# Talking-heads attention and squared-ReLU FFN: other anchors for the q, k and v loads, the first k by SP, some pre-mixing units in row tiles, and a new order of TensorE's units

## Chip, cores and metric

One core of one Trainium2 chip. The metric is the device time of one launch in microseconds (us), as the median of the runs shown; lower is better. Beside these runs stands one profiled execution, whose own time is given with its span.

## What is computed

Attention over 8 batches, 12 heads, 448 positions and a head size of 64, with the heads mixed before the softmax (`w_pre`) and after it (`w_post`), then a feed-forward layer with a squared ReLU on the 3584 x 768 result:

```python
scores = scale * np.matmul(q, k.transpose(0, 1, 3, 2))
scores = np.einsum('bhij,hg->bgij', scores, w_pre)
scores = scores - np.max(scores, axis=-1, keepdims=True)
attn = np.exp(scores)
attn = attn / (np.sum(attn, axis=-1, keepdims=True) + 1e-09)
attn = np.einsum('bhij,hg->bgij', attn, w_post)
return np.matmul(attn, v).astype(np.float32)
...
h = np.maximum(x @ w_in, 0.0)
return (h * h @ w_out).astype(np.float32)
```

Inputs and output are float32; the kernel computes in bfloat16 with float32 sums.

## The kernel before

**The stages of a batch.** q and k come from DRAM as bfloat16 (POOL's queue, `load_qk`, L624, two DMAs of half the partitions for each of three head groups `a` and each of q and k), and TensorE transposes them (`emit_T`, L710; "T" units). QK units (`emit_QK`, L859) give the scores of 128 query rows at a time, which ACT or DVE evict into `stage`; SP's DMAs (`emit_rel`, L918) regroup them in `dring` so that 10 query rows times 12 heads lie on the partitions. A pre-mixing unit (`emit_pre`, L940) multiplies two such groups by the block-diagonal `wk1`; ACT takes the exponentials with row sums into `pring` (L965), DVE the reciprocals, POOL folds them into the post-mixing weights (L986) and the tail (L1001). A post-mixing unit (`emit_post`, L1014) gives the mixed and transposed attention, evicted into `a2t`. AV units (`emit_AV`, L1092) multiply by v, F1 units (`emit_F1`, L1163) and F2 units (`emit_F2`, L1282) are the feed-forward layer. The output leaves from `osb` by POOL's queue, except the last two tiles (`emit_last`, L1242), which leave by SP and ACT.

**Batch 0 is different.** The first 22 groups of 10 rows skip regrouping and pre-mixing: DVE multiplies the transposed q by the mixing weights (`emit_scale`, L788; the products lie in `w_out_sb` and `h2t`, not yet in use), and "direct" units (`emit_direct`, L814) make mixed scores at once. Until 60 us, TensorE's gaps are partly filled by matmuls on a constant (`warm_up`, L587).

**TensorE's tiles.** A matmul uses the whole array ("full"), two tiles of 64 rows ("row"), two of 64 columns ("cols") or four of 64 x 64 ("quad"). Pre-mixing and T units are quad, post-mixing units and most QK units row, AV units cols, direct units full; F1 and F2 are row or full by a string each. In a pre-mixing unit each of the four tiles runs one 448-column matmul at the same time as the others.

**What sets the order.** The whole program is planned ahead: `_Plan` (L108) gives each task an engine and a place in that engine's queue. TensorE's units stand in ten streams (0 T, 1 QK, 2 pre-mixing, 3 post-mixing, 4 AV, 5 direct, 6 and 7 F1, 8 and 9 F2), and the string `ORDER` (L32), 948 digits long, says from which stream the next unit comes. All other tasks are placed by estimated costs and by a priority. A dependency in `deps` becomes a semaphore wait; one in `after` only keeps the planner from issuing a task before another, and leaves no wait in the program. The loads of batch b >= 2 are tied in this way to pre-mixing units (`emit_load_qk`, L678, and `emit_load_v`, L695, by `pre_at`): the twelve q and k loads to every second group from group 2 of batch b - 1, the six v loads to every second group from group 8 of batch b itself. The raw buffers are single, so each load also waits for the T unit of the batch before. The planner's constants (`FETCH` for instruction fetches of TensorE, `MODE_SWITCH`, `MARGIN` for the time kept free behind a transfer) enter nothing but its estimates.

Of the kernel before, what the change touches and what calls it, by code (L numbers as in the profile page):

```python
# [8 lines left out]
DT = mybir.dt  # L9
# [9 lines left out]
MODE_SWITCH = 106.0  # L19
ACT_BIAS = 14.5  # L20
BLOCK = 256
FETCH = (110e3, 6000.0, 4600.0, 1400.0)
# [6 lines left out]
MARGIN = {("move", PE): (0.0, 700.0), ("move", FLEX): (700.0, 1500.0),  # L29
          ("load", PE): (0.0, 900.0)}  # L30
INF = float("inf")
ORDER = (  # L32
    "0010155055051505511551555115555113553155550033555555550105555555311553332550220555315551"
    "2313332431244123622317667223677313361372267113667313242244137611376713127721266676623336"
    "7277128310028323839139229839200223444132622008111811181338317222167663123776313673132621"
    "4431411367217127766327621002677622383383338162267720028332677102208311813181338314212442"
    "2229391139313933922291444229119116316337221763363372217620016733722631620027137383200281"
    "1181118222939133911393124222441183138311831382224442216363372217633637212763362002277200"
    "2611637337339200292219119118131813183318222444223931193139331922244422881383138336221672"
    "1276200167337136336222772002736316720209119313922193831183138113822244422381381338224442"  # L40
    "2816336117117336221673373621167200226731362002713783382228382002911392219139393319222931"
    "9318338111811382224444442236171163377331722166662227637336372127922198338392298333832244"
    "42228876323267886673363363676787774448687787766676697767689989889999"
# [3 lines left out]
QK_QUAD = "001000000001000000000000000000000000000000001001000000010000001000000000000000000000000000000000000000000000000000000000000000000000000000000000000000000000000"  # L47
POST_QUAD = "0000000000000000000000000000000000000000000000000000000000000000000000000000000000000000000000000000000000000000000000000000000000000000000000000000000000000000000000000000000001100000"

# [58 lines left out]
class _Plan:  # L108
# [191 lines left out]
    def next_unit(self, order, at):  # L300
# [8 lines left out]
        if t.mode != self.mode:  # L309
            est = max(est, self.free[PE] + MODE_SWITCH)  # L310
# [41 lines left out]
def bass_talking_heads_attention__then__ffn_squared_relu_kernel(  # L352
# [45 lines left out]
    with ExitStack() as es:  # L398
# [883 lines left out]
        def emit_F2(b, tile, s, s_F):  # L1282
# [10 lines left out]
            if b == B - 1 and tile >= 2:  # L1293
                emit_last(b, tile, s, s_F, _Group(2), reads)
                return
# [185 lines left out]
```

## Time and profile before

| | |
|---|---|
| runs | 518.51, 519.75, 520.62 us; median 519.75 |
| profiled execution | 520.99 us, of it 519.3 us span |
| granted TensorE clock | 1.0 |
| TensorE (PE) busy | 506.3 us, 98% of the span |
| ACT, DVE, POOL busy | 434.1, 401.9, 268.4 us |
| DMA | 72.33 MB moved, HBM read 47.27 MB |

The profile names engines PE (matmuls), PEld (weight loads, overlapped), DVE, ACT, POOL and SP; a line such as L948 is a line of the kernel. "idle before" is the time an engine stood still ahead of an instruction, with the one that ended it. In the view of windows, each row is a stretch of the span, followed by the busy time of each engine and its number of instructions, the granted clock, the mean busy share of 16 DMA engines and GB/s. In a timeline, a row is a start, a length, an engine, a line and what was done, with equal neighbours merged.

### The profile page before, as it was taken

To read this page: it belongs to the slowest core of one execution; us is meant where nothing else is said; L and a number is where in the kernel's file an instruction comes from. 1 tells how busy PE (TensorE), PEld (TensorE's weight loads), DVE (VectorE), ACT (ScalarE), POOL (GpSimd) and SP (SyncE) were. 2 spreads that over 40 slices of the span, in tenths; PEclk is the share of its full clock that TensorE was granted. 3 is DMA by queue.
4 is the path that set the end of the run, shared out by engine and by line. 5 is a ranking of instruction groups with operands and counts; after the bars stand their busy time and mean duration, and the time that the engine had idled before them with its cause. 6 is when DMAs were issued, how large, how long until landed. Compare 5 with 4: busy or idle time off the path is not lost.

```text
span 519.3 us, 22377 instructions
## 1 busy us (share of the span) xinstructions
PE 506.3 (98%) x9169; PEld 319.7 (62%) x9169; DVE 401.9 (77%) x1025; ACT 434.1 (84%) x1256; POOL 268.4 (52%) x571
## 2 busy tenths in 40 slices
PE   7999899999999999999999999999999999999997
PEld 3455677567776664567455664566545665568884
DVE  8998999689979769888988869886896668755220
ACT  4989999799999898988888889888998888987531
POOL 9956556443673576244864459235664344443000
PEclk9999999999999999999999999999999999999999
DMA  8999999846895689646993679626995466551013
GB/s 112 196 227 193 199 180 189 168 115 136 157 190 135 142 174 187 124 97 141 173 186 76 142 156 197 148 66 152 174 166 119 102 154 120 103 118 32 1 32 93
DMA packets 83022, 72.33 MB, mean 139 GB/s; under 512 B 7160, under 2 KB 80424, under 8 KB 82920
## 3 DMA queue, kind: packets, MB, share of 16 engines
q0 software_dynamic: 37632, 33.83, 40.4%
q1 hardware_dynamic: 45000, 36.86, 29.0%
q8 instruction: 74, 1.21, 0.9%
q14 instruction: 28, 0.23, 0.1%
q10 hardware_dynamic: 288, 0.20, 0.1%
HBM read 47.27 MB, written 11.01 MB: 112 GB/s over the span
## 4 chain that ended last, share of the span: by engine, by line
PE 73%; DVE 12%; ACT 8%; DMA 3%; issue 2%; POOL 2%; POOLq 0%; ACTq 0%; DVEq 0%
PE ps L1311 23%; PE ps L1184 10%; PE ps L1176 10%; PE ps L1120 6%; PE ps L948 6%; PE ps L879 5%; PE ps L1036 5%; ACT pring L965 4%; PE ps L1303 3%; DVE stage L487 3%; DVE a2t L487 2%; PE ps L1251 2%; DMA kraw<-in_k_dram 2%; DVE w_out_sb L802 2%; PE ps L726 2%; ACT stage L486 2%
## 5 line engine op out<-in xcount | busy, mean ns | idle before, releaser
L965 ACT ACTIVATE pring<-ps 128x448 bf16<-128x448 f32 x360 | 191.7, 557 | 11.7 <-PE ps L948 9.4
L986 POOL TENSOR_TENSOR wk2s<-wk2b,rinv 128x120 bf16<-128x120 bf16 (+1 forms) x179 | 73.2, 409 | 145.7 <-DVE rinv L979 144.3
L487 DVE CAST a2t<-ps 128x420 bf16<-128x420 f32 (+1 forms) x208 | 124.8, 643 | 16.5 <-PE ps L1050 15.9
L1311 PE MATMUL ps<-w_out_sb,h2t 64*128 64x384 bf16 x1472 | 134.3, 323 | 0.3 <-ACT pring L965 0.2
L487 DVE CAST stage<-ps 128x448 bf16<-128x448 f32 (+1 forms) x179 | 107.3, 615 | 14.1 <-PE ps L879 12.8
L486 ACT ACTIVATE a2t<-ps 128x420 bf16<-128x420 f32 (+1 forms) x160 | 94.9, 645 | 13.1 <-PE ps L1050 12.8
L486 ACT ACTIVATE stage<-ps 128x448 bf16<-128x448 f32 (+1 forms) x181 | 94.8, 557 | 12.9 <-PE ps L879 12.2
L1311 PEld LDWEIGHTS ps<-w_out_sb,h2t 64*128 64x128 bf16 x1472 | 67.6, 94 | 45.3 <-issue 2.4
L1184 PE MATMUL ps<-xt,w_in_sb 64*128 64x448 bf16 (+1 forms) x840 | 88.4, 347 | 1.3 <-issue 1.1
L1348 POOL DMA_DIRECT2D out_dram<-osb x52 | 33.4, 648 | 93.3 <-ACT osb L486 30.7
L965 ACT ACTIVATION_READ_ACCUMULATOR pring<-ps 128x1 f32 x360 | 80.0, 222 | 0.0
L1176 PE MATMUL ps<-xt,w_in_sb 128*128 128x228 bf16 (+2 forms) x636 | 75.0, 270 | 1.0 <-ACT a2t L486 0.8
L1223 DVE TENSOR_TENSOR h2t<-h1t 128x448 bf16<-128x448 bf16 (+2 forms) x176 | 56.0, 341 | 20.2 <-ACT h1t L1213 17.1
L1001 POOL TENSOR_TENSOR ptail<-pring,rinv 128x128 bf16<-128x128 bf16 x171 | 70.2, 410 | 0.0
L1176 PEld LDWEIGHTS ps<-xt,w_in_sb 128*128 128x128 bf16 x636 | 58.2, 98 | 13.9 <-ACT a2t L486 1.7
L1036 PEld LDWEIGHTS ps<-wk2s,pring 60*128 60x128 bf16 (+1 forms) x2184 | 48.9, 94 | 24.7 <-issue 2.6
L1184 PEld LDWEIGHTS ps<-xt,w_in_sb 64*128 64x128 bf16 x840 | 37.5, 94 | 34.8 <-issue 2.2
L1213 ACT ACTIVATE h1t<-ps 128x448 bf16<-128x448 f32 (+2 forms) x100 | 43.5, 445 | 16.6 <-PE ps L1176 7.6
L1036 PE MATMUL ps<-wk2s,pring 60*128 60x60 bf16 (+1 forms) x2184 | 55.3, 187 | 1.3 <-ACT h1t L1213 0.6
L948 PE MATMUL ps<-dring,wk 64*64 64x448 bf16 (+1 forms) x676 | 54.0, 362 | 0.9 <-DVE a2t L487 0.3
L979 DVE RECIPROCAL rinv<-rowsum 128x2 f32<-128x2 f32 (+1 forms) x184 | 29.0, 157 | 32.9 <-ACT pring L965 31.5
L879 PE MATMUL ps<-qkt 64*128 64x448 bf16 (+1 forms) x372 | 51.1, 353 | 0.4 <-DVE qkt L487 0.3
(62 smaller groups left out, 564.1 us busy)
## 6 DMA issues: line engine op xcount, KB each, us to landing
dring<-stage SPq DMA_DIRECT2D x309, 105.0 KB
out_dram<-osb POOLq DMA_DIRECT2D x52, 192.0 KB, 4.0
vraw<-in_v_dram POOLq DMA_DIRECT2D x48, 128.0 KB
qraw<-in_q_dram POOLq DMA_DIRECT2D x48, 112.0 KB, 5.4
kraw<-in_k_dram POOLq DMA_DIRECT2D x48, 112.0 KB, 5.3
w_in_sb<-in_moe_w_in_dram POOLq DMA_DIRECT2D x8, 384.0 KB, 18.0
w_out_sb<-in_moe_w_out_dram POOLq DMA_DIRECT2D x8, 384.0 KB, 17.3
dring<-stage SPq DMA_DIRECT2D x30, 42.0 KB
```

The lines of the kernel that those rows point to most:

```text
L486: return eng.activation(o, i_, AF.Copy)
L487: return eng.tensor_copy(o, i_)
L879: r_ = eng.matmul(ps[y * v:(y + 1) * v, g.banks[x], 0:S], qkt[r0:r0 + 64, pp, 0, j0:j0 + v], qkt[r0:r0 + 64, pp, 1 + pb, :], start=True, s ...
L948: r_ = eng.matmul(ps[64 * y:64 * y + 64, gr.banks[x], 0:S], wk1[64 * x:64 * x + 64 - R0 * x, :], dring[64 * x:64 * x + 64 - R0 * x, (g0 + ...
L965: return eng.activation(pring[:, pr, 0:S], ps[:, gr.banks[x], 0:S], AF.Exp, accum_out=rowsum[:, pr, :])
L986: return eng.tensor_tensor(wk2s[:, p0:p0 + n, :], i0.to_broadcast([128, n, PR]), rinv[:, p0:p0 + n, :].to_broadcast([128, n, PR]), ALU.mult)
L1001: return eng.tensor_tensor(ptail[:, p0 // 2, :, :], pring[:, p0:p0 + 2, 0:PJ], rinv[:, p0:p0 + 2, :].to_broadcast([128, 2, PJ]), ALU.mult)
L1036: r_ = eng.matmul(ps[z * v:(z + 1) * v, gr.banks[x], o0:o0 + PR], pring[64 * x:64 * x + PR, pr + y, c:c + v], wk2s[64 * x:64 * x + PR, pr ...
L1176: r_ = eng.matmul(ps[:, gs[ph].banks[0], 0:n], w_in_sb[:, ft, t * 128:(t + 1) * 128], xt[:, ft, c0:c1], start=(ft == 0), stop=(ft == NFT - 1))
L1184: r_ = eng.matmul(ps[:, gs[0].banks[x], 0:n], w_in_sb[64 * y:64 * y + 64, ft, t * 128:(t + 1) * 128], xt[64 * y:64 * y + 64, ft, c0:c1], s ...
L1223: return eng.tensor_tensor(h2t[:, t16, o0:o0 + n], h1t[:, s, 0:n], h1t[:, s, 0:n], ALU.mult)
L1311: r_ = eng.matmul(ps[:, gs[0].banks[hh], 0:FH], h2t[64 * y:64 * y + 64, t16, col:col + 128], w_out_sb[64 * y:64 * y + 64, t16, hh * FH:(hh ...
```

## The change

- **Loads.** The q and k loads of batches 3 to 7 are tied to every second group from group 36 of batch b - 2 (46 group numbers a batch), so twelve groups earlier; batch 2 keeps its anchors. The v loads of batches 1 to 7 are tied to every third group from group 12 of their batch in place of every second from group 8.
- **First k.** Head group 0 of k of batch 0 no longer comes by POOL's queue with conversion on the way. SP issues two DMAs of float32 into the space of `pring` ahead of its other work, and ACT converts them into `kraw` (task "round").
- **Pre-mixing in row tiles.** For the units marked in `PRE_ROW` the same product is made by two passes of row tiles: each pass runs two 64-row tiles on 448 columns, the second adding to the first, with weights padded by zeros (`wk1z`). Ten units are marked: three of batch 0, three of batch 1 and one each of batches 2 to 5.
- **End.** The last output tile is cut in three instead of two: 384 columns, then twice 192, each with its own PSUM bank, eviction and two DMAs.
- **Plan.** `ORDER` and `QK_QUAD` (seven units in place of six) are new; `F1_FULL`, `F2_FULL` and `POST_QUAD` are the same. The planner's constants change: costs of a unit, of a change of tile mode, margins behind transfers, and a further one for fetches while several loads are in flight.

```diff
-MODE_SWITCH = 106.0
+MODE_SWITCH = {"quad": 119.0, "cols": 121.0, "row": 105.0, "full": 105.0}
-FETCH = (110e3, 6000.0, 4600.0, 1400.0)
+FETCH = (110e3, 6000.0, 4000.0, 5300.0, 1300.0)
-MARGIN = {("move", PE): (0.0, 700.0), ("move", FLEX): (700.0, 1500.0),
-          ("load", PE): (0.0, 900.0)}
+MARGIN = {("move", PE): (300.0, 1300.0), ("move", FLEX): (1000.0, 2200.0),
+          ("load", PE): (0.0, 1800.0)}
...
-        z = (at - self.fetched - FETCH[1 if at < FETCH[0] else 2]) / FETCH[3]
+        late = 1 if at < FETCH[0] else 3 if len(self.moving["load"]) > 1 else 2
+        z = (at - self.fetched - FETCH[late]) / FETCH[4]
...
+        def load_first_k():
+            wide = pring.bitcast(DT.float32)[:, 0:4, :].rearrange("p a b -> p (a b)")
+            ts = []
+            for u in range(2):
+                def fn(eng, en, u=u):
+                    i_ = bass.AP(k.tensor, u * NP * S * D, [[NT * D, PJ], [S * D, 2], [1, NT * D]])
+                    eng.dma_start(wide[64 * u:64 * u + 64, :].rearrange("p (a b) -> p a b", a=2),
+                                  i_).then_inc(sem_k.handle, 16)
+
+                ts.append(plan.add("ldk%d" % u, SP, fn, [], {SP: (420.0, 0.0)}, -2e6 + u,
+                                   sem_k, 16, dma=("load", 350.0, 88.0)))
+
+            def fn_round(eng, en):
+                o = kraw[:, 0:2, :, :].rearrange("p a t d -> p (a t d)")
+                return eng.activation(o, wide, AF.Copy)
+
+            t = add("round", ACT, fn_round, ts, {ACT: (985.0, 1135.0)}, -5e6)
+            return [t, t]
...
+                    if (b, a, x) == (0, 0, 1):
+                        ts += load_first_k()
+                        continue
...
-                            after = [chain["t"], pre_at((b - 1) * NCP + 2 + 2 * n)]
+                            g0 = (b - 1) * NCP + 2 if b == 2 else (b - 2) * NCP + 36
+                            after = [chain["t"], pre_at(g0 + 2 * n)]
...
-                after = [qk_tasks[(1, 2)][-1]] if b < 1 else [pre_at(b * NCP + 8 + 2 * n)]
+                after = [qk_tasks[(1, 2)][-1]] if b < 1 else [pre_at(b * NCP + 12 + 3 * n)]
...
+                if row:
+                    for y in (1, 0):
+                        for x in range(len(gs)):
+                            rows = slice(64 * x, 64 * x + 64 - R0 * x)
+                            c0, m = (0, 128) if y else (64, 66)
+                            r_ = eng.matmul(ps[0:m, gr.banks[x], 0:S], wk1z[rows, c0:c0 + m],
+                                            dring[rows, (g0 + y) % NDS, :],
+                                            start=y == 1, stop=True, skip_group_check=True)
+                    return r_
...
-            for hh in range(2):
-                for q0 in range(0, NFFT, nk):
+            spans = [(0, 0, 2, nk), (1, 2, 2, nk)]
+            if tile == 3:
+                spans = [(0, 0, 2, nk), (1, 2, 1, NFFT), (2, 3, 1, NFFT)]
+            for i, y0, ny, nu in spans:
+                w = ny * OP
...
-                emit_last(b, tile, s, s_F, _Group(2), reads)
+                emit_last(b, tile, s, s_F, _Group(tile), reads)
```

## What is predicted, before the changed kernel ran

> **What bounds the kernel now.** I read the profile by stages first, since TensorE's 98% is a mean over stages with different limits.
>
> ```profile
> 0.00:6.00 6.00, 4.54 (x42) 2.00 (x42) 4.20 (x10) 2.46 (x3) 4.84 (x13) 1.00 0.55 78
> 6.00:15.00 9.00, 7.33 (x183) 3.30 (x169) 8.67 (x23) 5.35 (x11) 8.99 (x16) 1.00 1.06 143
> 15.00:35.00 20.00, 20.00 (x269) 9.91 (x268) 19.92 (x52) 17.60 (x50) 16.43 (x23) 1.00 1.26 216
> 35.00:65.00 30.00, 27.85 (x525) 17.57 (x523) 26.56 (x71) 28.53 (x89) 17.99 (x40) 1.00 1.12 199
> 65.00:200.00 135.00, 133.56 (x2586) 92.64 (x2580) 113.32 (x305) 123.94 (x374) 77.72 (x168) 1.00 0.79 160
> 200.00:330.00 130.00, 127.70 (x2541) 75.75 (x2537) 111.70 (x272) 114.32 (x325) 71.41 (x156) 1.00 0.74 148
> 330.00:515.00 185.00, 184.65 (x3060) 118.31 (x3050) 117.53 (x299) 141.44 (x407) 71.05 (x159) 1.00 0.48 103
> 515.00:519.30 4.30, 0.71 (x5) 0.20 (x2) 0.00 (x0) 0.49 (x1) 0.00 (x0) 1.00 0.35 92
> ```
>
> The first number after the stretch is its length, the next TensorE's busy time, then weight loads, DVE, ACT, POOL, the clock, the DMA share and GB/s. TensorE's idle time is the difference of the first two: 1.46 and 1.67 us before 15 us, none from 15 to 35, 2.15 from 35 to 65, 1.44 to 200, 2.30 to 330, 0.35 to 515 and 3.59 in the tail, 12.96 in all. So better waiting can save at most some 13 us, and after 330 us almost nothing: there each nanosecond of added TensorE work adds to the end. Between 6 and 35 us DVE is full as well (28.59 of 29 us), though TensorE looks busy with matmuls on a constant among the rest.
>
> Next the start, by the timeline, and the chain of waits across it.
>
> ```profile
> 0.81 0.40 SPq L556 DMA_DIRECT2D wall<-in_w_pre_dram  x1
> 2.65 1.22 POOL L630 DMA_DIRECT2D kraw<-in_k_dram  x2
> 4.15 1.25 POOL L630 DMA_DIRECT2D qraw<-in_q_dram  x2
> 5.68 0.30 PEld L726 LDWEIGHTS ps<-ident,qraw 64*64 64x64 bf16 x28 [0.37 <-DMA qraw<-in_q_dram]
> 7.67 0.30 PEld L726 LDWEIGHTS ps<-ident,kraw 64*64 64x64 bf16 x28 [1.34 <-DMA kraw<-in_k_dram]
> 14.04 0.30 PEld L726 LDWEIGHTS ps<-ident,kraw 64*64 64x64 bf16 x28 [0.37 <-DMA kraw<-in_k_dram]
> ...
> 7.08 5.29 DMA qraw<-in_q_dram
> 13.28 1.70 DVE w_out_sb L802 x3
> ```
>
> The six tensors of batch 0 arrive one after the other: first q transposed at 5.68, last k at 14.04, that is (14.04 - 5.68) / 5 = 1.67 us apiece. The chain runs through POOL's issues and such a landing until 12.37 us and through DVE from there. The input transfers pace the first 12 us, DVE the next 23.
>
> **The change part by part.** *First k by SP.* The nearest rows for its price are SP's transfer of 72 KB and an ACT copy of as many columns:
>
> ```profile
> wall<-in_w_pre_dram SPq DMA_DIRECT2D x1, 72.0 KB, 3.4
> L486 ACT ACTIVATE qkt<-ps 128x896 bf16<-128x896 bf16 x5 | 4.6, 912 | 0.0
> ```
>
> Each of the two new loads is 64 x 2 x 1792 bytes, 229 KB. They stand first on SP, so the second is issued at 0.81 + 0.40 = 1.21 us. From below it lands like the 72 KB, at 4.6; from above 459 KB at the 216 GB/s of the busiest stretch add 2.1 us, 6.7. I take 5.3. ACT converts in some 0.91 us and is free (2.46 of 6 us busy), so k is ready at 5.5 to 7.6, most likely 6.2, and its transposes start then in place of 7.67. The matrix of mixing weights, queued behind on SP, is issued 0.8 us later; its first user on DVE comes only after 6 us, and it lands by 0.81 + 0.8 + 3.4 = 5.0, so it costs nothing. POOL issues 1.22 us less ahead of the second q, and one of six places in the row of landings is gone: the last input is there up to 1.67 us sooner. DVE has only 0.33 us idle in 6 to 15, so the gain comes through only as far as ACT (3.65 us idle there) takes over evictions. Ends 0 and -1.67; I take **-1.2**, near the second, as the chain has transfers until 12.37.
>
> *Loads of batches 3 to 7.* The first row is the landing of k's DMAs over the whole run (minimum, median, maximum).
>
> ```profile
> DMA to landing us min/median/max: 3.7/5.3/12.1
> 256.35 0.61 POOL L630 DMA_DIRECT2D kraw<-in_k_dram  x1
> 256.95 0.65 POOL L641 DMA_DIRECT2D vraw<-in_v_dram  x1
> 257.57 0.63 POOL L630 DMA_DIRECT2D kraw<-in_k_dram  x1
> 267.25 0.30 PEld L726 LDWEIGHTS ps<-ident,kraw 64*64 64x64 bf16 x28 [0.57 <-DMA kraw<-in_k_dram]
> ...
> 105.51 2.41 PE ps L1120 x60
> 257.57 9.63 DMA kraw<-in_k_dram
> ```
>
> Today q, k and v loads alternate on POOL, since their anchors overlap; a k issued at 257.57 landed 9.63 us later and TensorE stood 0.57 us. In the order string the last anchor of batch 3's third pair is 15 units ahead of its use; 948 units in 515 us are 0.54 us each, so that is 8 us, under the maximum of 12.1. With the new string the same distance is 41 units, 22 us. The waits on the raw buffers stay met: the T unit that frees one stands at least 36 units ahead of the new anchor in each of the batches 3 to 7, so nothing queued behind these loads on POOL (folds and tails, for which post-mixing waits) is held up by them. The number of DMAs stays but for the two of the first k. v's last anchor comes nearer to its first AV unit: 20 units (11 us) or more in batches 2 to 7, but in batch 1 it is 10 units, 5.4 us, where it was 29; the AV work of batch 1 is the row at 105.51. If that landing is like k's median it just fits (see the last rival). So **-0.5**, between -0.6 and the +6.7 of that rival.
>
> *Stalls without a cause in the program.* Twice TensorE stood in the middle of an F1 unit, both times while loads had just been issued:
>
> ```profile
> 205.66 0.63 POOL L630 DMA_DIRECT2D qraw<-in_q_dram  x1
> 206.83 0.30 PEld L1184 LDWEIGHTS ps<-xt,w_in_sb 64*128 64x128 bf16 x5 [1.18 <-issue]
> 256.69 0.68 PEld L1184 LDWEIGHTS ps<-xt,w_in_sb 64*128 64x128 bf16 x10 [0.45 <-issue]
> q8 instruction: 74, 1.21, 0.9%
> ```
>
> No semaphore ended them, and the instruction queue moved 1.21 MB in 74 pieces, 16 KB each, so I read them as late instruction blocks behind load traffic. The two are 1.63 us; new anchors move them or end them. I take **-0.8**, ends -1.6 and +1.5 (as many again). The Trainium skill, "Runtime: NRT & Kernel Launch", section "Instruction fetch mechanics", has the fetch of 16 KiB blocks run ahead unseen; by it these stalls would be something else, the term 0 and the sum 0.8 worse. The 16 KB pieces agree, the stalls in mid-unit do not.
>
> *Pre-mixing in row tiles.* A quad unit between two full ones, and what row tiles would cost:
>
> ```profile
> 85.42 1.34 PE L1176 MATMUL ps<-xt,w_in_sb 128*128 128x228 bf16 x12 [0.16 <-ACT pring L965]
> 86.69 0.38 PE L948 MATMUL ps<-dring,wk 64*64 64x448 bf16 x4
> 87.00 1.34 PE L1176 MATMUL ps<-xt,w_in_sb 128*128 128x228 bf16 x12
> ...
> 56.23 2.37 PE ps L1176 x24
> 207.96 1.14 PE ps L1184 x12
> ```
>
> From start to start of the F1 units pass 1.58 us; their 12 matmuls take 2.37 / 2 = 1.19, so the quad unit with both changes of mode costs 0.39 to 0.40. Six pairs of 448-column row matmuls take 1.14, 0.19 a pass, and two passes 0.38. In the best place a row unit gains 0.02; where its neighbours are not both row it loses up to 0.19. Counted over the two order strings, changes of mode fall from 254 to 250: at (0.39 - 0.19) / 2 = 0.10 each that is -0.4, against ten more passes, +1.9. So the new string holds up to +1.5 us more TensorE work than the old, if all else is equal; six of the ten units lie in batches 0 and 1, where there is idle time to take them. I put **+0.6**, ends -0.2 and +1.5.
>
> *Order searched anew.* The idle time that is left between 35 and 330 us is 2.15 + 1.44 + 2.30 = 5.89, less the 0.57 and 1.63 above: 3.7, mostly waits for evictions. I can't replay the order; a fifth of it gives **-0.8**, ends -2.5 and +1.5.
>
> *End.*
>
> ```profile
> 507.75 7.96 PE L1251 MATMUL ps<-w_out_sb,h2t 128*128 128x384 bf16 x48
> 515.75 0.49 ACT L486 ACTIVATE osb<-ps 128x384 f32<-128x384 f32 x1 [1.76 <-PE ps L1251]
> 516.27 0.64 ACTq L1274 DMA_DIRECT2D out_dram<-osb  x1
> L486 ACT ACTIVATE xt<-ps 128x220 bf16<-128x220 f32 x36 | 11.0, 374 | 2.1 <-PE ps L1120 1.4
> out_dram<-osb ACTq DMA_DIRECT2D x2, 96.0 KB, 2.5
> L1251 PEld LDWEIGHTS ps<-w_out_sb,h2t 128*128 128x128 bf16 x64 | 6.3, 98 | 4.0
> ```
>
> A 384-column matmul takes 7.96 / 48 = 0.166; 32 of half the columns are 2.65 us, as much as the 16 they replace. The last eviction falls from 0.49 to about 0.35 (between the 220 and 384 columns, carried on), -0.14, and half of 96 KB lands a little sooner than 2.5, say -0.15. **-0.3**, ends -0.6 and +0.4 (the first rival).
>
> Sum: -1.2 - 0.5 - 0.8 + 0.6 - 0.8 - 0.3 = **-3.0**. The profiled execution took 520.99 us (519.3 span and 1.7 around it), so 518.0 of its kind; it lay 1.24 above the median 519.75, and by the median I forecast **516.8**.
>
> **Rivals.**
> *Weight loads set the tail's pace.* Each of the 32 short matmuls brings its own 128-column weight load. For: one is busy 98 ns, more than 83. If they can't overlap, the two last pieces take 32 x 0.099 = 3.17 in place of 2.65, the end term is +0.2 and the time 517.3. Against: weight loads overlap already, and no row shows them as the limit. The Trainium skill, "TensorE: Matmul & The Clock Gate", section "LDWEIGHTS (loading the stationary operand)", has 128 columns take 107 ns; by that pace the pieces would need 3.4 us. The 24 matmuls in 2.37 us, 0.099 with a weight load each, are already faster. Chance 0.04.
>
> *DVE hides the start, and the order gives nothing.* DVE's work from 6 to 35 us starts with the first q, which isn't earlier; full as it is, the first k gains nothing, the searched order only pays for its passes. Then -0.5 - 0.8 - 0.3 + 0.6 = -1.0, and 518.7; the planner can shift evictions to ACT, which speaks against it. With part of the start the case reaches 517.3. Chance 0.33.
>
> *The loads do what they did, elsewhere.* The waits at 206.8, 256.7 and 267.3 only move, the start and the end gain: 519.75 - 1.2 - 0.3 + 0.6 - 0.8 = 518.0. Chance 0.07.
>
> *Slower: the last v of batch 1 is late.* Its load is issued some 5.4 us ahead of the first AV unit, in a stretch with DMA at 0.79 and the batch's own output and q, k loads of batch 2 about. No row has v's landing; if it takes the 12.1 of k's worst, TensorE stands 12.1 - 5.4 = 6.7 us at about 105 us, as every unit behind AV waits in the same queue: 516.8 + 6.7 = 523.5. It decides from a landing of 5.4 + 3.0 = 8.4 us on, where the whole sum is used up; the 9.63 above would do. Against it: the median is 5.3, and the units between may be longer than the mean. Chance 0.13.
>
> **How the numbers follow.** The forecast has 0.43, the rivals in their order 0.04, 0.33, 0.07 and 0.13. About 0.5% (2.6 us) is what a measurement of this kernel can tell from no change: faster means below 517.15. The forecast's own range, its ends taken in part, is 513.8 to 518.3, and nearly all of it below 517.15 holds 0.45 with the first rival's share; the cases of 517.3 to 518.7 and the mild end of the last are within 0.5%, 0.43; slower (over 522.35) is the rest of the last, 0.12. The range 513.8 to 521.0 takes in all but that and what lies below 513.8.
>
> **What would show it.** First k's transposes at 6 to 7 us and the last input before 13 (if the DVE chain still starts its scaling work at the same pace, the second rival). No wait for kraw after 60 us, and no wait of over 0.4 us without a releaser inside an F1 unit; idle of 35 to 330 us near 4 in place of 5.9. Ten pre-mixing units of 0.38 us with 128-column tiles, and a tail after the last matmul of 3.3 in place of 3.6. A wait for vraw near 105 us, or a TensorE busy sum above 507 us, would make the forecast wrong.

## The result, and the profile after

| | before | after |
|---|---|---|
| median of the runs | 518.85 us (six runs, 518.33 to 520.62) | 524.06 us (six runs, 521.87 to 526.48) |
| profiled execution, its span | 520.99, 519.3 | 523.35, 521.5 |
| TensorE busy | 506.3 | 509.9 |
| granted TensorE clock, runs | 1.0 (profiled run) | 0.997, 0.993, 1.0, 0.997, 0.997, 0.999 |

The ratio is 1.0092, 95% interval 1.0069 to 1.0115: the change made the kernel slower by 0.9%, where 516.8 us was forecast. The profiled executions show 2.4 of the 5.2 us, as the one of before lies above its median and the one of after below.

The stretches of the changed kernel, in the same view as for the kernel before (length, busy time of TensorE, weight loads, DVE, ACT, POOL, then the granted clock):

```profile
0.00:6.00 6.00, 4.54 (x13) 1.88 (x14) 4.20 (x10) 2.46 (x3) 4.79 (x13) 1.00 0.65 124
6.00:15.00 9.00, 7.30 (x194) 3.22 (x192) 7.65 (x21) 5.49 (x11) 9.00 (x18) 1.00 1.17 177
15.00:35.00 20.00, 20.00 (x269) 9.93 (x268) 19.65 (x52) 18.54 (x52) 12.82 (x19) 1.00 1.26 214
35.00:65.00 30.00, 29.30 (x518) 18.48 (x516) 25.67 (x72) 29.44 (x90) 18.41 (x41) 1.00 1.08 195
65.00:200.00 135.00, 131.51 (x2506) 90.95 (x2506) 111.46 (x300) 118.98 (x359) 75.85 (x163) 0.99 0.79 152
200.00:330.00 130.00, 129.18 (x2554) 77.06 (x2551) 112.49 (x274) 115.53 (x325) 70.26 (x154) 1.00 0.77 149
330.00:515.00 185.00, 184.60 (x3107) 118.94 (x3106) 120.58 (x306) 143.89 (x418) 73.97 (x164) 1.00 0.54 106
515.00:521.50 6.50, 3.50 (x38) 2.96 (x35) 0.00 (x0) 1.24 (x4) 0.00 (x0) 1.00 0.36 91
```

Idle time (length less busy time) fell from 12.96 us to 11.57: 35 to 65 us has 0.70 in place of 2.15, 200 to 330 us 0.82 in place of 2.30. But 65 to 200 us has 3.49 in place of 1.44, and TensorE's busy sum rose by 3.6 us. Busy time can rise without more work: six matmuls of a direct unit that take 1.31 us at a granted clock of 1.00 (run h5 below, at 13.75 us) take 2.39 at 0.50 (run e3, at 14.07). Half clock is what follows the largest new wait, first in the timeline, then in the chain of work, last in the windows around it:

```profile
153.25 11.81 SPq L952 DMA_DIRECT2D dring<-stage  x10
162.93 0.38 PE L986 MATMUL ps<-dring,wk1z 64*64 64x448 bf16 x4 [2.17 <-DMA dring<-stage]
```

```profile
155.00 7.68 DMA dring<-stage
```

```profile
155.00:160.00 5.00, 5.00 (x124) 3.94 (x112) 4.64 (x16) 5.00 (x20) 3.95 (x9) 1.00 0.88 160
160.00:165.00 5.00, 2.83 (x78) 1.58 (x76) 2.36 (x8) 2.71 (x10) 1.79 (x5) 0.85 0.65 144
165.00:170.00 5.00, 5.00 (x88) 3.03 (x86) 3.19 (x6) 2.99 (x6) 0.54 (x2) 0.81 0.49 94
170.00:175.00 5.00, 5.00 (x112) 3.63 (x110) 4.68 (x10) 4.50 (x14) 1.85 (x3) 1.00 0.49 88
```

A pre-mixing unit of batch 2 waited 2.17 us for its regrouped scores, and then the clock column falls under 1. From 163.49 to 166.90 us the granted clock is 0.50; (1 - 0.85) x 5 + (1 - 0.81) x 5 = 1.7 us of work were lost: 3.4 us at half speed. This wait is paid nearly twice.

The start, in the timeline and in the DMA view:

```profile
0.81 1.45 SPq L647 DMA_DIRECT2D pring<-in_k_dram  x2
2.29 0.60 SPq L560 DMA_DIRECT2D wall<-in_w_pre_dram  x1
7.14 0.30 PEld L753 LDWEIGHTS ps<-ident,qraw 64*64 64x64 bf16 x28 [1.07 <-DMA qraw<-in_q_dram]
7.35 0.32 PEld L753 LDWEIGHTS ps<-ident,kraw 64*64 64x64 bf16 x28
7.74 0.44 DVE L568 TENSOR_SCALAR wq<-wall 64x72 f32<-64x72 f32 x2 [1.19 <-DMA wall<-in_w_pre_dram]
8.96 0.66 PE L906 MATMUL ps<-qkt 64*128 64x448 bf16 x4 [0.70 <-DVE qkt L491]
9.23 1.23 DVE L829 TENSOR_TENSOR w_out_sb<-qkt,wq 128x480 bf16<-128x480 bf16 x2
```

```profile
pring<-in_k_dram SPq DMA_DIRECT2D x2, 224.0 KB, 4.1
wall<-in_w_pre_dram SPq DMA_DIRECT2D x1, 72.0 KB, 5.4
```

The mixing weights (`wall`) are issued 1.48 us later and take 5.4 us to land in place of 3.4; DVE, in whose queue the step that needs them stands ahead of its evictions, waits for them, and its first scale product starts at 9.23 in place of 7.32. The first k is ready sooner (transposes at 7.35, not 7.67), but the first q later (7.14, not 5.68).

The tail: the last eviction starts at 518.53 of 521.5 us, 3.0 us from the end, where it was 515.75 of 519.30, 3.55.

```profile
518.53 0.33 ACT L490 ACTIVATE osb<-ps 128x192 f32<-128x192 f32 x1 [0.99 <-PE ps L1294]
```

### The profile page after: what moved, and what is told of

Same layout as the page of the kernel before. It is cut to its first block, busy times and chain, and to the rows that moved or that the text cites. A ratio compares the mean times of both kernels' runs of the same rounds, so it can differ in the third digit from the quotient of the medians.

```text
span 521.5 us, 22405 instructions
## 1 busy us (share of the span) xinstructions
PE 509.9 (98%) x9186; PEld 323.4 (62%) x9186; DVE 401.7 (77%) x1028; ACT 435.6 (84%) x1255; POOL 265.1 (51%) x569
## 4 chain that ended last, share of the span: by engine, by line
PE 80%; DVE 9%; ACT 6%; DMA 3%; POOL 1%; issue 1%; SPq 0%
PE ps L1355 23%; PE ps L1223 13%; PE ps L1215 9%; PE ps L1159 6%; PE ps L986 6%; PE ps L1075 5%; PE ps L906 5%; PE ps L851 4%; PE ps L1347 3%; ACT pring L1004 3%; DVE stage L491 3%; PE ps L1294 2%; PE ps L753 2%; DVE a2t L491 2%; DMA dring<-stage 1%; DVE h2t L1262 1%
## 5 line engine op out<-in xcount | busy, mean ns | idle before, releaser
L1355 PE MATMUL ps<-w_out_sb,h2t 64*128 64x384 bf16 x1472 | 135.9, 324 | 0.8 <-PE ps L1089 0.4
L491 DVE CAST a2t<-ps 128x420 bf16<-128x420 f32 x206 | 122.3, 639 | 17.1 <-PE ps L1089 16.5
L491 DVE CAST stage<-ps 128x448 bf16<-128x448 f32 (+1 forms) x181 | 108.9, 615 | 15.4 <-PE ps L906 13.4
L490 ACT ACTIVATE a2t<-ps 128x420 bf16<-128x420 f32 (+1 forms) x162 | 96.8, 654 | 15.5 <-PE ps L1089 15.3
L490 ACT ACTIVATE stage<-ps 128x448 bf16<-128x448 f32 (+1 forms) x179 | 93.7, 559 | 10.4 <-PE ps L906 10.0
L986 PE MATMUL ps<-dring,wk1z 64*64 64x448 bf16 (+1 forms) x636 | 51.6, 363 | 3.1 <-DMA dring<-stage 2.2
```

The source lines that it names most:

```text
L490: return eng.activation(o, i_, AF.Copy)
L491: return eng.tensor_copy(o, i_)
L986: r_ = eng.matmul(ps[64 * y:64 * y + 64, gr.banks[x], 0:S], wk1[64 * x:64 * x + 64 - R0 * x, :], dring[64 * x:64 * x + 64 - R0 * x, (g0 + ...
L1355: r_ = eng.matmul(ps[:, gs[0].banks[hh], 0:FH], h2t[64 * y:64 * y + 64, t16, col:col + 128], w_out_sb[64 * y:64 * y + 64, t16, hh * FH:(hh ...
```

## The experiments

Theory at the outset: the loss has two places, the late `wall` of the start and the regrouping move that comes late in batch 2 because q and k loads were moved next to it. Rival: the new order itself has no room there, whatever the loads do.

### One part taken back from the changed kernel

**q, k anchors as before** (e1):

```diff
-    g0 = (b - 1) * NCP + 2 if b == 2 else (b - 2) * NCP + 36
+    g0 = (b - 1) * NCP + 2
```

> The changed kernel with the old anchors for the q and k loads of batches 3 to 7 (every second group from group 2 of the batch before), all else as changed. Theory M (the earlier q, k loads slow SP's regrouping moves of batch 2, one lands late, TensorE stands 2.2 us at 163 us and its clock then halves for 3.4 us): the wait is gone, no half clock, about 519 to 520 us. Theory V (the later v loads delay the move) and theory O (the new order asks for the move too early by itself): the wait stays, 523 to 525 us.

527.97 us, ratio 1.0154 (1.0122 to 1.0185). The move is no longer waited for, as theory M has it, but k is, in the list of waits, and the time rose:

```profile
PE ps L753 <- DMA kraw<-in_k_dram: 5.8, 1, 5.8
```

**v anchors as before** (e2), and **both as before** (e3, with the edit of e1 too):

```diff
-    else [pre_at(b * NCP + 12 + 3 * n)]
+    else [pre_at(b * NCP + 8 + 2 * n)]
```

> The changed kernel with the old anchors for the v loads (every second group from group 8), all else as changed. Theory V (the two v loads and the output stores issued at 154 to 157 us delay the moves issued at 154 to 155): the wait at 163 us is gone, about 519 to 520 us. Theories M and O: it stays, 523 to 525 us.

e2: 524.01 us, 1.0083 (1.0056 to 1.0111), no different from the changed kernel. The wait for the move is gone, which is theory V's sign, and its profiled execution (522.36, the shortest of its six) shows no half clock before the last matmul, yet the time isn't the 519 to 520 that V expected. A unit stands in its middle instead, with no semaphore as releaser, and a 16 KB packet of the instruction queue is in flight between 149.0 and 150.2 us and none from there to the end of the stall:

```profile
151.63 1.15 PE L1355 MATMUL ps<-w_out_sb,h2t 64*128 64x384 bf16 x12 [2.09 <-issue]
```

```profile
q8 instruction: 1, 0.02, 4.7%
```

> The changed kernel with the old anchors for q, k and v. Theory O (the order alone leaves pre-mixing too close behind its moves): still a wait of 1 us or more on a regrouping move in batch 2, 523 us or more. Theories M and V, alone or together: no such wait, 518 to 520 us.

e3: 524.11 us, 1.008 (1.0052 to 1.0108): taking the anchors back buys nothing. The time is theory O's, the sign is nobody's: TensorE waits for no move between 130 and 170 us, but stands there 0.9 us without a releaser and 0.8 for k, and at the start its profiled execution was at half clock for 6.8 us.

**The old order, no row tiles** (e4):

```diff
-ORDER, QK_QUAD of the change
+ORDER, QK_QUAD of the kernel before
-PRE_ROW = "000000000000001100000100000000000001010010000000...
+PRE_ROW = "000000000000000000000000000000000000000000000000...
```

> The changed kernel with the order string and the QK tile string of before and no pre-mixing unit in row tiles; new anchors, first k by SP, cut tail and planner constants stay. Theory O: no wait on a regrouping move, 517 to 519 us. Theories M and V: the anchors delay the moves under this order too, with a wait in batch 2 or 3, 521 us or more.

527.15 us, 1.0143 (1.0096 to 1.019): the old order with the new loads is no better than the new order with the old anchors (e3), and 3.1 us slower than the changed kernel. That refutes theory O's 517 to 519. The time is in M's and V's range, but no wait for a move is there; the longest between 130 and 170 us is 1.1 us, for DVE. The runs of before beside these four had a median of 519.35.

### One part added to the kernel before

Each kernel here is the one before with those lines of the change's diff that make up the part named; the runs of before beside them had a median of 519.24.

**First k by SP** (f1; `load_first_k` and the three lines that call it):

> The kernel before with one part of the change: first k of batch 0 by SP in float32 and converted by ACT. Theory S (the float32 loads delay the first q from 5.7 to 7.1 us, and the start is lost by that): first q's transposes at about 7 us, first AV unit of batch 0 about 1 us later than 49.6, 520 to 521 us against 519.3. As it was predicted blind (-1.2): 518.1. Theories A and C see the loss elsewhere: 519 to 520.

522.49 us, 1.0054 (1.0036 to 1.0071). The timeline shows the whole sequence, and the windows its second half:

```profile
8.33 0.76 DVE L565 TENSOR_SCALAR wq<-wall 64x72 f32<-64x72 f32 x2 [1.81 <-DMA wall<-in_w_pre_dram]
9.12 0.98 DVE L488 COPY qkt<-ps 128x448 bf16<-128x448 bf16 x3
9.87 0.56 PE L902 MATMUL ps<-qkt 64*128 64x448 bf16 x2 [2.02 <-DVE qkt L488]
10.14 1.23 DVE L825 TENSOR_TENSOR w_out_sb<-qkt,wq 128x480 bf16<-128x480 bf16 x2
```

```profile
9.80:13.20 3.40, 3.33 (x37) 1.28 (x37) 3.04 (x8) 2.38 (x5) 3.40 (x7) 0.50 1.26 196
```

DVE waits for `wall`, the evictions of q stand behind it, TensorE's first QK unit waits 2.02 us for them, and half clock follows for 3.4 us. The loss of 3.2 us is above what theory S expected (520 to 521).

**The anchors** (f2; `load_qk` from group `(b - 2) * NCP + 36`, `load_v` from `b * NCP + 12 + 3 * n`):

> The kernel before with the new anchors of q, k and v loads alone, on the old order. Theory A (the anchors cost: loads then run beside regrouping moves and instruction fetches that the order was fitted around): 522 to 526 us, with a wait of over 1 us between 100 and 165 us. As it was predicted blind: the wait for k at 267 us is gone, 518.5 to 519. Theories S and C: 519 to 520.

521.82 us, 1.005 (1.0036 to 1.0063): slower, if a little under theory A's range, and without its sign. TensorE's longest wait between 100 and 165 us is 0.4 us.

**The planner's constants** (f3) and **the split tail** (f4):

> The kernel before with the new constants of the planner alone (mode changes, fetch, margins, unit costs): TensorE's order is the same, but ACT's, DVE's and the queues' tasks are placed anew. Theory C (these placements no longer fit the order: evictions come in another sequence): 521 to 526 us. Theories A and S: within 1 us of 519.3.

> The kernel before with the last output tile cut in three. Predicted blind: 0.3 us less, 519.0 against 519.3, the last eviction 0.35 us instead of 0.49; by the rival (weight loads pace the short matmuls) 0.2 us more, the 32 short matmuls in 3.2 us instead of 2.65.

519.58 us, 1.0001 (0.9987 to 1.0015), and 518.91 us, 0.9992 (0.9978 to 1.0006). Neither differs from before by more than the interval.

### The start and the anchors, taken apart

**`wall` first on SP, ahead of the two k loads** (g1 on the kernel f1, g2 on the changed kernel):

```diff
-    t_wall = plan.add("wall", SP, fn_wall, [], {SP: (400.0, 3300.0)}, -1e6 - 1, sem_wq, 16)
+    t_wall = plan.add("wall", SP, fn_wall, [], {SP: (400.0, 3300.0)}, -3e6, sem_wq, 16)
```

> The kernel before with the first k by SP as in f1_first_k, but the 72 KB matrix of mixing weights stands first on SP again, ahead of the two k loads. Theory 'the matrix came late': f1's loss of 2.8 to 3.3 us came from DVE's first scale matrices waiting 1.81 us for it, with all evictions behind them; here they start by 6.9 us, the first scale product by 7.8 (before 7.32, f1 10.14), and the time is 518 to 519.8, ratio 0.997 to 1.001. Rival 'the two float32 k loads themselves hold up the first q': the first q's transposes stay at 6.7 us (before 5.69) and the time is 520.5 to 522, ratio 1.002 to 1.005. Rival 'a start in another order of arrivals throws TensorE out of step and its clock falls': as f1, 1.005 or more.

521.49 us, 1.0032 (1.001 to 1.0055): about 1 of the 3.2 us back, with overlapping intervals, and in the range of the second expectation. `wall` is on time, but now q and k are not:

```profile
6.44 0.40 DVE L565 TENSOR_SCALAR wq<-wall 64x72 f32<-64x72 f32 x2
7.17 0.41 PE L749 MATMUL ps<-ident,qraw 64*64 64x64 bf16 x28 [1.37 <-DMA qraw<-in_q_dram]
8.33 0.41 PE L749 MATMUL ps<-ident,kraw 64*64 64x64 bf16 x28 [0.76 <-ACT kraw L652]
```

The k transposes come at 8.33, after the 7.67 of the kernel before, so SP's load gains nothing at all there. This profiled execution took 525.15 us, well above its median, with a wait of 2.6 us near 21 us that need not stand for the others; only its first 10 us are used for the price of the start.

> The changed kernel with the matrix of mixing weights first on SP. Theory 'the matrix came late': DVE's wait of 1.19 us for it before 8 us is gone, the first scale product starts a microsecond sooner than 9.23, and the time falls by 1 to 2 us against the 524.06 of the changed kernel: 522 to 523, ratio to before 1.005 to 1.008; the wait for a regrouping move near 161 us and the half clock behind it stay. Rival 'nothing of the start reaches the end': 524, 1.009. Rival 'the planner's evictions, placed anew, only move the stalls': 523 to 526, with a new wait of over 1 us somewhere between 130 and 300 us.

525.02 us, 1.0103 (1.0069 to 1.0137): no gain, the third of the expectations. The first scale product starts at 7.39, but the k transposes at 8.53.

**q, k anchors alone** (g3) and **v anchors alone** (g4) on the kernel before, one line of f2 each; before had 519.38 beside g1 to g4:

> The kernel before with the new anchors of the q and k loads alone (v as before). f2 with both cost 2.6 us. Theory 'q, k loads brought forward collide with regrouping moves and with fetched code between 100 and 170 us': most of it is here, 520.7 to 522, ratio 1.003 to 1.005, and the median move around 120 to 160 us lands later than before. Rival 'v's late loads do it': 519 to 519.8, 0.999 to 1.001.

> The kernel before with the new anchors of the v loads alone (q, k as before). Theory 'q, k loads brought forward do it': 519 to 519.8, ratio 0.999 to 1.001; a wait for v near 105 us isn't there. Rival 'v's late loads do it' (they then fall on the next batch's q, k loads): 520.7 to 522, 1.003 to 1.005.

523.33 us, 1.0066 (1.0044 to 1.0088), and 520.41 us, 1.0029 (1.0008 to 1.005). q and k carry most of the loss, with TensorE's order unchanged, and more than was expected: 3.9 us alone and v's 1.0, where both together cost 2.6 (f2). So the parts don't add here either. The loss of g3 is spread: 130 to 170 us has 1.11 us of idle time, 200 to 330 us 2.51. One piece of it is on POOL, where two q loads and a v load now stand directly ahead of folds and tails (its timeline):

```profile
249.28 1.25 POOL L630 DMA_DIRECT2D qraw<-in_q_dram  x2
250.51 0.63 POOL L641 DMA_DIRECT2D vraw<-in_v_dram  x1
251.15 0.41 POOL L987 TENSOR_TENSOR wk2s<-wk2b,rinv 128x120 bf16<-128x120 bf16 x1
251.50 0.41 POOL L1002 TENSOR_TENSOR ptail<-pring,rinv 128x128 bf16<-128x128 bf16 x1
...
252.05 0.34 PE L1037 MATMUL ps<-wk2s,pring 60*128 60x60 bf16 x12 [0.73 <-POOL ptail L1002]
252.74 0.34 PE L1037 MATMUL ps<-wk2s,pring 60*128 60x60 bf16 x12 [0.32 <-POOL ptail L1002]
```

### The new order by itself

The first k, the anchors and the split tail, each added to the kernel before, sum to 3.2 + 2.6 - 0.3 = 5.5 us, yet in the changed kernel taking them back gains little. So the order had to be priced alone.

**The changed kernel with the first k by POOL** (h1), and **with the anchors as before too** (h4), which leaves order, row tiles, constants and tail:

```diff
-    if (b, a, x) == (0, 0, 1):
-        ts += load_first_k()
-        continue
```

> The changed kernel with the first k loaded by POOL as before (all else as changed). On the kernel before, the first k by SP cost 3.2 us (f1) and 2.1 with the matrix first (g1). Theory 'the first k by SP costs in the new order as well': the matrix lands in time, DVE's first scale product is back near 7.3 us (9.23 in the changed kernel), the first half clock and idle of the start are gone, and the time is 521 to 522.6, ratio 1.003 to 1.0065. Rival 'the new order was laid out round that load and has taken its cost in': 523.5 to 525, 1.008 to 1.011.

> The changed kernel with the first k by POOL and all anchors as before: what is left of the change is the new order, row tiles, constants and the tail. By the prediction's terms (-0.8 + 0.6 - 0.3) 518.8, ratio 0.999. Theory 'the new order itself brings nothing; without its anchors k comes late in it': the wait for k of e1 or the fetch stalls of e3 near 160 us return, 521 to 525. If it is 520 or below, the first k and the anchors are the whole loss.

h1: 523.14 us, 1.0068 (1.0054 to 1.0083). h4: 523.82 us, 1.0096 (1.0073 to 1.0119). h1 lies between its two expectations (522.6 and 523.5). In h4 the order and its row units, with every load as before, cost 4.6 us against the 519.25 of its own comparison, nearly the whole loss; constants and tail by themselves were within their intervals (f3, f4). Idle time between 130 and 170 us, first the split tail on the old order (f4), then h4, then h1, each by its window and, for the last two, followed by its longest wait there:

```profile
130.00:170.00 40.00, 39.72 (x830) 28.85 (x826) 35.34 (x93) 37.76 (x117) 23.47 (x50) 1.00 0.81 161
```

```profile
130.00:170.00 40.00, 37.91 (x793) 27.41 (x792) 33.92 (x91) 37.33 (x113) 24.36 (x53) 1.00 0.82 158
```

```profile
PE ps L750 <- DMA kraw<-in_k_dram: 1.2, 1, 1.2
```

```profile
130.00:170.00 40.00, 38.30 (x804) 28.39 (x804) 35.39 (x97) 36.78 (x114) 20.85 (x47) 1.00 0.74 142
```

```profile
PE ps L983 <- DMA dring<-stage: 1.5, 1, 1.5
```

0.28 us with the old string, 2.09 and 1.70 with the new one: with the loads as before k is late, with the loads brought forward the regrouping move is.

This is not the whole of h4's loss, nor the larger part in its profile. The sums of its page, then those of f4 and of h1 (spans 521.0, 516.6 and 520.0 us, clock 1.0 in all three until the last matmul):

```profile
PE 510.8 (98%) x9190; PEld 323.7 (62%) x9190; DVE 401.2 (77%) x1026; ACT 438.2 (84%) x1256; POOL 265.3 (51%) x571
```

```profile
PE 507.1 (98%) x9185; PEld 320.7 (62%) x9185; DVE 401.5 (78%) x1026; ACT 433.4 (84%) x1256; POOL 268.5 (52%) x571
```

```profile
PE 508.2 (98%) x9190; PEld 323.1 (62%) x9190; DVE 401.6 (77%) x1028; ACT 436.2 (84%) x1254; POOL 266.5 (51%) x571
```

Of the 4.4 us that h4's span is longer than f4's, 3.7 are in TensorE's busy sum and 0.7 in its idle time: what 130 to 170 us lost, other stretches gave back in part. h1 runs the same units in the same order and has 1.1 us more busy time than f4 and 2.3 more idle. So the busy sum moves by 2.6 us without any change of units, and how much of it is the ten further passes can't be read from it.

**No row tiles** (h2, the `PRE_ROW` of e4) and **q, k brought forward by half as much** (h3), both in the changed kernel:

```diff
-    g0 = (b - 1) * NCP + 2 if b == 2 else (b - 2) * NCP + 36
+    g0 = (b - 1) * NCP + 2 if b == 2 else (b - 2) * NCP + 42
```

> The changed kernel with no pre-mixing in row tiles (all quad). The prediction's term: ten units cost 0.6 us (-0.2 to +1.5), so without them 523.5 (522.5 to 524.3). Rival 'the ten units pay for changes of mode beside row units': without them up to 2 us slower, 524.5 to 526. Rival 'which stall falls where decides, not the units': a change of over 1 us either way with a wait of over 1 us in another place between 130 and 310 us.

> The changed kernel with the q, k anchors of batches 3 to 7 brought forward by six groups in place of twelve. With none (e1) TensorE waited 5.8 us for k at 161 to 167 us and the time was 527.97; with twelve, 2.17 us for a regrouping move at 163 us, and 524.06. Theory 'loads forward push the regrouping moves, loads back push k': in between both waits are under 1 us, and the time is 520.5 to 523. Rival 'the stall between 130 and 170 us belongs to the new order, whatever the anchors': a wait of 1 us or more is there again in another place, and the time is 523.5 to 527.

525.28 us, 1.0118 (1.0105 to 1.0131), and 524.67 us, 1.0104 (1.0078 to 1.013). Without the ten units the kernel isn't faster, with a wait of 2.0 us for a move between 130 and 170 us and half clock at the start: whatever their passes cost is outweighed by waits, since everything is planned anew around them. Halfway, neither k nor the move is waited for, and a wait of 1.2 us for DVE's reciprocals stands in the same stretch; the start of its profiled execution again has half clock. So the idle time there, 1.7 to 6.6 us, comes with the new string whatever the loads do. It isn't the string alone: with the old string the stretch has 0.28 us in the kernel before, but 1.1 to 2.3 with loads moved (f2, g3, g4, e4).

**Old string in places 278 to 364 of the changed kernel** (h5), and **new string in places 182 to 247 of f4** (h6); the edit of h5, and that of h6 is of the same kind:

```diff
-    "1124411343217672166771227672002723833832383183366200227662137720028311831383118314212442"
-    "2192239313911391391192319224442291633633722176336372127602016733722613620027373183200281"
+    "1124411343217127766327621002677622383383338162267720028332677102208311813181338314212442"
+    "2229391139311391391192319224442291633633722176336372127602016733722613620027373183200281"
```

> The changed kernel with the old order string put back in places 278 to 364 of 948 alone (some 137 to 181 us; the two strings have the same units up to both ends). In all kernels with the new string TensorE is idle for 1.7 to 6.6 us between 130 and 170 us, each time by another wait; in the kernel before 0.28. Theory 'the new string's sequence there has too little room between a group's QK unit, its regrouping and its pre-mixing': the idle time of 130 to 170 us falls under 1 us, no wait for a regrouping move or for k, and the time is 520.5 to 522.3 (524.06 less 2 to 3.5). Rival 'the head of the program shifts evictions and transfers so that some wait falls there with either string': 523.3 to 526, with a wait of over 1 us between 130 and 170 us.

523.81 us, 1.0089 (1.0069 to 1.011). The place is cured, the time is not:

```profile
6.00:15.00 9.00, 6.99 (x136) 2.96 (x134) 5.85 (x17) 4.36 (x8) 8.30 (x17) 0.81 1.15 170
...
130.00:170.00 40.00, 39.11 (x806) 28.73 (x806) 34.99 (x95) 37.51 (x118) 20.99 (x47) 1.00 0.75 144
```

Idle time of 130 to 170 us falls to 0.89, as the theory has it. But in this execution the start has half clock, after a wait of 2.0 us for DVE, worth (1 - 0.81) x 9 = 1.7 us. The six runs spread from 522.01 to 525.61, the two at clock 1.0 being the fastest, 522.01 and 522.67; elsewhere clock 1.0 is no such sign (the changed kernel's run at 1.0 took 524.77). So the place is confirmed and its price isn't: the median missed the expected 520.5 to 522.3.

> The kernel before with the split tail (f4) and the new order string in places 182 to 247 alone (some 87 to 122 us), where idle time of 85 to 105 us is 1.02 us in f4 and 0.09 in the changed kernel. Theory 'a local piece of the searched order keeps its gain': 517.5 to 518.6, ratio to before 0.9965 to 0.9985. Rival 'the gain depends on what goes ahead, or is given back by a stall later on': 518.8 to 522, with a new wait of over 0.5 us after 105 us.

522.39 us, 1.0053 (1.0036 to 1.0071): slower than f4, on which it builds. The rival held. The gain of that stretch isn't kept, and a stall without a releaser falls due 80 us behind its end, with half clock after it (timeline, window). The execution with this stall took 525.02 us and is the slowest of the six, so it need not stand for the others:

```profile
203.53 0.74 PE L1184 MATMUL ps<-xt,w_in_sb 64*128 64x448 bf16 x6 [2.08 <-issue]
```

```profile
204.00:208.00 4.00, 4.00 (x31) 1.31 (x28) 1.95 (x5) 2.31 (x9) 1.02 (x3) 0.58 0.84 173
```

No version beat the kernel before by more than its interval; the split tail alone, 518.91, is the only one that isn't slower by the median.

## Why the prediction was wrong, step by step

Slower was held for 0.12, by a late v of batch 1. That isn't what happened: no wait for v appears in the changed kernel. The steps, in the order of their weight:

- **Order searched anew, -0.8 (-2.5 to +1.5): the failed step.** With its row units, for which the prediction added 0.6, it was to gain 0.2; together they measured +4.6 with every load as before (h4). No run has the order without them on the old loads, so the two aren't priced apart. The step took a fifth of the remaining idle time as a gain, and allowed for a loss no larger than the extra passes. It didn't ask what a unit that is moved forward will wait for. What the runs show in its place is that idle time doesn't only shrink: between 130 and 170 us it rose from 0.28 us to 1.7 to 6.6 in every kernel with the whole new string, for k (e1, h4) or for regrouped scores (the changed kernel, h1, h2) that land later than the string asks for them, in h3 for reciprocals and in e2 without a releaser. The old string there took the idle time away (h5) and not the loss, so it is not shown that this is all of the 4.6 us. The prediction measured the room of loads in units (15 before, 41 after); the room between a regrouping move and its pre-mixing unit it didn't measure at all.
- **First k by SP, -1.2 (0 to -1.67): wrong in sign.** +3.2 on the kernel before (f1); in the changed kernel 0.9 (h1 against 524.06), which the intervals don't separate from nothing. The step said that `wall`, queued behind on SP, "costs nothing", as it would land at 5.0. It took the 3.4 us landing of an empty start, and two 224 KB loads ahead of it made that 5.4 to 6.0. The rest, with `wall` in time (g1, +2.1 over before), goes with q and k that land later in the fuller start; g1's own profile is no guide to where its last microsecond went, so that stays open.
- **Loads, -0.5 (-0.6 to +6.7): wrong in sign on the old order.** The wait for k near 267 us is gone, as forecast: no wait for k after 60 us. Yet on the kernel before the new anchors cost 2.6 (f2), q and k alone 3.9 (g3). The statement that nothing behind these loads on POOL is held up considered their semaphores alone; the issues themselves take 0.63 us each, and post-mixing waited 1.05 us for the tails behind them. In the new order the anchors are worth -0.7 (h1 against h4, within the intervals); there they exchange the wait of 1.2 us for k for one of 1.5 us for a move.
- **Row tiles, +0.6.** The ten units are there, and the price of two passes came out in six of the ten, where the next unit starts 0.37 to 0.38 us after the row unit, as forecast (the view's 0.54 us runs to the end of the last matmul); in the other four it starts 0.42 to 0.53 us after. One of the six, and the unit behind it, in the changed kernel:

```profile
98.90 0.54 PE L980 MATMUL ps<-dring,wk1z 64*128 64x448 bf16 x4
99.28 1.46 PE L1355 MATMUL ps<-w_out_sb,h2t 64*128 64x384 bf16 x16
```

What they are worth to the whole isn't separated: without them the changed kernel was 1.2 us slower (h2).
- **Stalls without a cause, -0.8 (-1.6 to +1.5).** The two at 206.8 and 256.7 us are gone from the changed kernel's profile, more than the half that the term took, but stalls of 2.1 us of the same kind came up in e2 and h6. No run prices the term by itself.
- **End, -0.3.** The tail after the last eviction's start is 0.55 us shorter in the changed kernel's profile, but in that of f4, which has the split tail alone, it is 3.6 us (512.97 to 516.6), no shorter than before. f4 measured -0.3 against its comparison, within its interval. Not contradicted, and not shown.

The text's own markers: a TensorE busy sum above 507 us was to make the forecast wrong, and it is 509.9; but f3 and f4, which aren't slower, have 507.4 and 507.1, so that mark alone would have misled. Idle time of 35 to 330 us is 0.70 + 3.49 + 0.82 = 5.01, where 4 was forecast and 5.9 was there before. The first k's transposes come at 7.35 us, not at 6 to 7, and the last input's at 13.2, not before 13.

One cost had no term in the sum: the clock. The mean of the six granted clocks is 0.9972, so some 0.28% of 521 us, 1.5 of the 5.2 us, was lost at half clock; behind which waits is known for the profiled execution alone. The 27 runs of the kernel before, in the comparison for f1 to f4, show no clock under 0.999, though beside e1 to e4 the lowest is 0.996.

What stays open is why the parts don't add up. First k, anchors and order (with its row units) cost 3.2, 2.6 and 4.6 us alone and 5.2 together. The runs show that a stall moves to another place rather than ends, and that old order with new loads (e4) and new order with old loads (h4, e3) are both slow; that order and loads have to fit each other is the reading of it, not shown by a run that makes them fit.

## What to carry to other kernels

Where TensorE is busy for 98% and the idle time is already down to tenths of a microsecond, a new order is not priced by the idle time that it could save, but by what each moved unit will wait for: list the landing of its operands, moves within the chip as well as loads, and the distance left to each. A load that is put first on a queue delays all that stands behind it by more than its issue, through the landing time; look for the engine whose first queued instruction needs the next one. And a wait of about 2 us can cost nearly 4, when half clock follows; the next section shows on what that hung here.

## What the runs showed of the hardware

- **Half clock after short waits.** In these twenty profiles half clock ahead of the last matmul comes in pieces of 3.41 us, seven times one and twice two (e1, e3), and a piece filled with work costs 1.7 us. The length of the wait didn't decide: half clock followed waits of 1.75 us (e3), 2.0 (f1, h3, h5), 2.1 (h6), 2.2 (the changed kernel), 2.6 (g1) and 5.8 (e1), and in h2 two gaps of 1.2 and 0.3 us, but not waits of 2.1 us in e2 and 2.0 in h2. Counting off 3.41 us from where the clock falls, the idle time of TensorE within the one such stretch just ahead sorts them: 3.41 us (e1), 2.41 (g1), 2.29 (h3), 2.17 (the changed kernel), 2.08 (h6), 2.01 (h5), 1.98 (f1), then 1.63 (e3) and 1.43 (h2). e3 as an example (windows; TensorE's busy time stands behind the length, the granted clock is the third figure from the end):

```profile
6.05:9.47 3.42, 1.79 (x61) 0.73 (x59) 0.85 (x5) 1.49 (x2) 3.42 (x9) 1.00 1.14 170
9.47:12.88 3.41, 2.69 (x36) 1.33 (x37) 3.38 (x10) 2.10 (x5) 3.41 (x7) 0.50 1.19 174
```

The edges of the stretches lie on a fixed grid within an execution: in h2 the clock falls at 11.25 us and again, behind the last matmul, at 523.25, 512.00 apart, which is 150 times 3.4133. Counted back by such steps from where the clock of e2 falls behind its last matmul (519.50 us), an edge lies at 150.86, in the middle of its wait, with 1.33 us of idle time in the stretch ahead of it and 0.77 in the next:

```profile
147.45:150.86 3.41, 2.08 (x50) 1.29 (x45) 3.41 (x8) 3.24 (x10) 1.19 (x4) 1.00 0.93 176
150.86:154.28 3.42, 2.65 (x44) 1.88 (x45) 0.97 (x3) 0.94 (x2) 0.74 (x2) 1.00 0.63 170
```

The wait of 2.0 us in h2 is cut into 0.27 and 1.72 in the same way. So 1.98 us and more of idle time in one stretch was followed by half clock every time, 1.40 to 1.75 us in two of nine cases, less never. The Trainium skill, "TensorE: Matmul & The Clock Gate", section "Part 1: The HAM clock gate (the "warmup" mystery)", puts the return to half rate after at least one idle window of about 3.4 us, the window running free of the program. The length of the window and its running free of the program agree; it didn't have to be idle throughout here, as 1.43 to 2.41 of its 3.41 us were enough in all but e1.
- **Stalls that look like a late fetch.** Stalls of 2.08 and 2.09 us without a releaser stood in the middle of the program's straight line, each after one 16 KB packet of the instruction queue. That they are waits for that code is inferred from the two views together; with 74 such packets in some 520 us, one every 7 us, one can stand ahead of a stall by chance.
- **Landing under load.** The same 72 KB took 3.4 us alone at the start and 5.4 and 6.0 us behind 448 KB on the same queue, with the DMA engines' share from 0 to 6 us at 0.55 and 0.65.
